# Two PSUM banks held as one tile, nine-row loads of q and k, and evictions with a stride, in an attention kernel followed by a hard-swish MLP

## The chip, the cores and the metric

One core of a Trainium2 chip. The metric is device time in microseconds (us). The kernel before took 399.7 us as the median of its first three runs.

## The reference, cut to what matters

```python
# q, k, v: (8, 8, 576, 64); s: (8, 8, 576); w_in: (512, 2048); w_out: (2048, 512)
cum    = np.cumsum(np.maximum(s, 0.0), axis=-1)
bias   = -(cum[:, :, :, None] - cum[:, :, None, :])
scores = np.where(causal, -1e9, q @ k.T / 8 + np.minimum(bias, 0.0))
attn   = softmax(scores)
x      = (attn @ v).transpose(0, 2, 1, 3).reshape(4608, 512)
h      = x @ w_in
out    = (h * np.clip(h + 3.0, 0.0, 6.0) / 6.0) @ w_out
```

64 heads are worked on as 32 pairs. For a pair, q and k are cast and transposed (qT, kT); scores gives exp(q k) in Pm; attend multiplies it by v into O, and VectorE divides by the row sums (r, then xs); x_transpose puts xs into xT, the x of the MLP. Four pairs give x for one batch of 576 tokens. The MLP runs in 9 blocks of 512 tokens; a block has 16 tasks `m1` (h, then in two steps, trl and gT, the hard-swish) and 16 tasks `m2` (a quarter of an output tile each).

Of the kernel before, what the change touches and what calls it, by code (L numbers as in the profile page):

```python
# [16 lines left out]
def kernel(  # L17
# [21 lines left out]
    NF = DFF // 128  # L39
    NBLK = NT // 512  # L40
    GRAN = 10
    VW = D + 2
    PW = 1664
    SLOTW = W2 + 64
# [2 lines left out]
    cpool = ctx.enter_context(tc.tile_pool(name="consts", bufs=1))  # L47
    work = ctx.enter_context(tc.tile_pool(name="work", bufs=2))
    psum = ctx.enter_context(tc.tile_pool(name="psum", bufs=1, space=bass.MemoryType.PSUM))

    ident_dram = nc.inline_tensor(np.eye(128, dtype=np.float16), name="ident_f16")

# [64 lines left out]
    qk_f = {}  # L117
    qk_h = {}

    def load_qk(p, eng):  # L120
        b, h0 = (2 * p) // H, (2 * p) % H
        t = work.tile([128, NTR, 2, D], F32, tag="qkf", bufs=3, name=f"qkf{p}")
        for i, src in enumerate((q, k)):
            eng.dma_start(
                out=t[:, :, i, :],
                in_=src[b, h0:h0 + 2].rearrange("h s d -> (h s) d").rearrange(
                    "(t p) d -> p t d", p=128
                ),
            )
        qk_f[p] = t  # L130

    def load_v(p, eng):
# [17 lines left out]

    def cast_qk(p):
        t = work.tile([128, NTR, 2, D], F16, tag="qkh", bufs=2)
        nc.gpsimd.tensor_copy(out=t, in_=qk_f.pop(p))  # L153
        qk_h[p] = t

    def cast_v(p):
        sl = p % NS
        eng = nc.vector if p in (1, 2, 3, 4) else nc.gpsimd
        eng.tensor_copy(out=v_h[:, sl, :, :, 0:D], in_=v_f[:, sl])  # L159

    def banks(early):

        return dict(tag="M", bufs=2) if early else dict(tag="S", bufs=3)

    def transpose_group(p, g):
        t0, t1 = ((0, 5), (5, 9))[g]
        n = (t1 - t0) * 128
        pT = psum.tile([128, 640], F16, **banks(p < 5))
        src = qk_h[p]
        for t in range(t0, t1):  # L170
            nc.tensor.matmul(  # L171
                out=pT[:, (t - t0) * 128:(t - t0 + 1) * 128],
                lhsT=src[:, t, :, :],
                rhs=ident,
                is_transpose=True,
                start=(t == t0),
                stop=(t == t1 - 1),
            )
        sl = p % NS
        c0 = t0 * 128  # L180
        nc.vector.tensor_copy(out=qT[0:64, sl, c0:c0 + n], in_=pT[0:64, 0:n])  # L181
        nc.vector.tensor_copy(out=kT[0:64, sl, c0:c0 + n], in_=pT[64:128, 0:n])  # L182
        if g == 1:
            qk_h.pop(p)



# [92 lines left out]
    def x_transpose(p):  # L280
        b, hp = p // (H // 2), p % (H // 2)
        xs = x_tiles.pop(p)
        pX = psum.tile([128, 640], F16, **banks(p < 3))
        for qt in range(5):
            nc.tensor.matmul(  # L285
                out=pX[:, qt * 128:(qt + 1) * 128],
                lhsT=xs[:, qt, :, :],
                rhs=ident,
                is_transpose=True,
                start=(qt == 0),  # L290
                stop=(qt == 4),
            )
        nc.vector.tensor_copy(out=xT[:, hp, b * SEQ:(b + 1) * SEQ], in_=pX[:, 0:SEQ])  # L293


    def load_w_in(c):
        nc.gpsimd.dma_start(
            out=w_in_sb[:, :, c * 512:(c + 1) * 512],
            in_=moe_w_in[:, c * 512:(c + 1) * 512].rearrange("(kc p) f -> p kc f", p=128),
        )  # L300

    def load_w_out(c):
        nc.gpsimd.dma_start(
            out=w_out_sb[:, c * 4:(c + 1) * 4, :],
            in_=moe_w_out[c * 512:(c + 1) * 512, :].rearrange("(ft p) j -> p ft j", p=128),
        )


    gT = {}
# [2 lines left out]
    def m1(n, f):  # L312
        if f == 0:
            gT[n] = work.tile([128, NF, 512], F16, tag="gT", bufs=2, name=f"gT{n}")
        ph = psum.tile([128, 512], F32, tag="M", bufs=2)
        for kc in range(KC):
            nc.tensor.matmul(  # L317
                out=ph,
                lhsT=w_in_sb[:, kc, f * 128:(f + 1) * 128],
                rhs=xT[:, kc, n * 512:(n + 1) * 512],  # L320
                start=(kc == 0),
                stop=(kc == KC - 1),
            )
# [5 lines left out]

    def m2(n, t4, part):  # L330
        if part == 0:
            pouts[n, t4] = psum.tile([128, 512], F32, tag="Y", bufs=1, name=f"po{n}_{t4}")
        po = pouts[n, t4]
        for f in range(4 * part, 4 * part + 4):
            nc.tensor.matmul(  # L335
# [13 lines left out]
    nc.vector.memset(bias3, 3.0)  # L349


    load_qk(0, nc.sync)
    load_v(0, nc.scalar)
    load_qk(1, nc.sync)
    load_v(1, nc.sync)
    load_qk(2, nc.sync)
    load_v(2, nc.sync)
    mask_rows(0, nc.scalar.copy)
    nc.scalar.activation(out=qaug, in_=c8, func=AF.Copy, scale=-1.0)
    mask_rows(1, nc.scalar.copy)  # L360
    nc.scalar.dma_start(
        out=kaug_dram.rearrange("r (h t) -> h r t", h=NH), in_=kaug
    )
    nc.scalar.dma_start(out=qaug_dram.rearrange("r (h t) -> h (r t)", h=NH), in_=qaug)
    load_aug(0, nc.scalar)
    load_aug(1, nc.scalar)


    def keep_warm(n):
        pw = psum.tile([128, 512], F32, tag="M", bufs=2, name="pw")  # L370
        for i in range(n):
            nc.tensor.matmul(
                out=pw, lhsT=warm[:, 0:128], rhs=warm, start=(i == 0), stop=(i == n - 1)
            )

    weights = {
        1: [(load_w_in, 0)],
        2: [(load_w_in, 1), (load_w_in, 2)],
        3: [(load_w_in, 3)],
        4: [(load_w_out, 0), (load_w_out, 1)],  # L380
        5: [(load_w_out, 2), (load_w_out, 3)],
    }

    def att_tasks(p):


        def loads():
            if p + 2 < NP:
                load_aug(p + 2, nc.sync)
            if p + 3 < NP:  # L390
                load_qk(p + 3, nc.sync)
                load_v(p + 3, nc.sync)
            for load, c in weights.get(p, []):
                load(c)

        more = p + 1 < NP
        tasks = [(loads, 0)]
        for bi in range(4):
            tasks.append((lambda bi=bi: scores_bank(2 * p, bi), 400))
        if p > 0:  # L400
            tasks.append((lambda: attend(2 * p - 1), 1200))
        if more:
            tasks.append((lambda: transpose_group(p + 1, 0), 640))
        for bi in range(4):
            tasks.append((lambda bi=bi: scores_bank(2 * p + 1, bi), 400))

        def casts():
            if more:
                cast_v(p + 1)
            if p + 2 < NP:  # L410
                cast_qk(p + 2)

        tasks.append((casts, 0))
        if p > 0:
            tasks.append((lambda: x_transpose(p - 1), 640))
        if more:
            tasks.append((lambda: transpose_group(p + 1, 1), 512))
        tasks.append((lambda: attend(2 * p), 1200))
        return tasks

    def weave(att, mlp):

        total = float(sum(c for _, c in att)) or 1.0
        done = 0.0
        for i, task in enumerate(mlp):
            while att and done / total < i / len(mlp):
                a, c = att.pop(0)
                a()
                done += c
            task()  # L430
        for a, c in att:
            a()

    def m1_tasks(n):
        return [lambda f=f: m1(n, f) for f in range(NF)]

    def m2_tasks(n):
        return [lambda t4=t4, part=part: m2(n, t4, part) for t4 in range(4) for part in range(4)]

    def merged(a, b):  # L440

        out_ = []
        for t in range(4):
            f, g = a[4 * t:4 * t + 4], b[4 * t:4 * t + 4]
            out_ += [g[0], g[1], f[0], g[2], f[1], g[3], f[2], f[3]]
        return out_

    keep_warm(22)
    cast_qk(0)
    transpose_group(0, 0)  # L450
    transpose_group(0, 1)
    mask_rows(2, nc.vector.tensor_copy)
    cast_v(0)
    cast_qk(1)
    keep_warm(10)
    att_all = []
    cut = []
    for b in range(B):
        for p in range(4 * b, 4 * b + 4):
            att_all += att_tasks(p)  # L460
            if p % 4 == 0:

                cut.append(len(att_all) - 2)
    att_all += [(lambda: attend(NH - 1), 1200), (lambda: x_transpose(NP - 1), 640)]
    cut.append(len(att_all))
    att_of = [att_all[cut[b]:cut[b + 1]] for b in range(B)]
    for task, _ in att_all[:cut[1]]:
        task()

    weave(att_of[1], m1_tasks(0))  # L470
    for n in range(NBLK - 1):
        att = att_of[n + 2] if n + 2 < B else []
        weave(att, merged(m1_tasks(n + 1), m2_tasks(n)))
    for task in m2_tasks(NBLK - 1):
        task()


# [28 lines left out]
```

## The kernel before: what the change and the argument touch

```python
def banks(early):
    return dict(tag="M", bufs=2) if early else dict(tag="S", bufs=3)

def load_qk(p, eng):                    # rows t*128 + partition: 256 bytes each
    t = work.tile([128, NTR, 2, D], F32, tag="qkf", bufs=3)
    for i, src in enumerate((q, k)):
        eng.dma_start(out=t[:, :, i, :], in_=src[...].rearrange("(t p) d -> p t d", p=128))

def transpose_group(p, g):              # five tiles of 128 rows, then four
    t0, t1 = ((0, 5), (5, 9))[g]
    n = (t1 - t0) * 128
    pT = psum.tile([128, 640], F16, **banks(p < 5))
    # ... one transpose for each t in t0..t1 ...
    nc.vector.tensor_copy(out=qT[0:64, sl, c0:c0 + n], in_=pT[0:64, 0:n])
    nc.vector.tensor_copy(out=kT[0:64, sl, c0:c0 + n], in_=pT[64:128, 0:n])

def m1(n, f):
    ph = psum.tile([128, 512], F32, tag="M", bufs=2)      # one bank, one tile
    for kc in range(KC):                                  # four matmuls
        nc.tensor.matmul(out=ph, lhsT=w_in_sb[:, kc, f * 128:(f + 1) * 128],
                         rhs=xT[:, kc, n * 512:(n + 1) * 512], ...)
    trl = work.tile([128, 512], F32, tag="trl", bufs=3)
    nc.scalar.activation(out=trl, in_=ph, func=AF.Relu, bias=bias3[:, 0:1], scale=1.0)
    nc.vector.scalar_tensor_tensor(out=gT[n][:, f, :], in0=trl, scalar=6.0, in1=ph,
                                   op0=ALU.min, op1=ALU.mult)

def m2(n, t4, part):
    if part == 0:
        pouts[n, t4] = psum.tile([128, 512], F32, tag="Y", bufs=1)
    # ... four matmuls; after the fourth part VectorE scales into osb, and osb goes out ...
```

Cut: scores, softmax, attend, the cumulative rows, and the order in which tasks are emitted.

The softmax here doesn't subtract the row's maximum and nothing guards it: scores larger than these inputs give would overflow.

## Time and profile before

| stretch of the kernel before | us | what sets its length |
|---|---|---|
| start to the first scores | 16.1 | the cumulative rows come back from DRAM |
| to the first m1 | 28.9 (until 45.0) | attention alone, GpSimd's casts, then a wait for q/k |
| to the second stage (first m2) | 37.5 (until 82.5) | m1 of block 0 woven with attention, one more wait for q/k |
| to the end | 314.8 (until 397.3) | TensorE, busy without a break |

The table cuts the span at four instructions: the first scores matmul, the first m1 matmul, the first m2 matmul of the second stage (after the change, the first beyond the eight m2 tasks that are moved forward), and the end. Two views that the prediction does not show are needed later. First, the groups of instructions of the kernel before, those of one m1 (columns: line, engine, operation, output and inputs, form, count; then busy time and the mean of one in ns; then the engine's idle time just ahead of the group and what ended most of it):

```profile
L317 PE MATMUL ph<-xT,w_in_sb 128*128 128x512 f16 x576 | 147.4, 381 | 0.0
L325 ACT ACTIVATE trl<-ph,bias 128x512 f32<-128x512 f32 x144 | 99.6, 692 | 82.8 <-PE ph L317 81.0 <-DVE kT L182 1.7
L326 DVE SCALAR_TENSOR_TENSOR gT<-trl,ph 128x512 f16<-128x512 f32 x144 | 98.8, 687 | 114.7 <-ACT trl L325 114.5
...
L317 PEld LDWEIGHTS <-w_in_sb 128*128 128x128 f16 x576 | 52.2, 98 | 44.5 <-issue 1.1
```

The last field of the first line is the one to watch: TensorE (PE) never waits for anything ahead of an m1, though each m1 is followed by 0.69 us on ScalarE (ACT) and 0.69 us on VectorE (DVE) that both read its bank.

### The profile page before, as it was taken

To read this page: it belongs to the slowest core of one execution; us is meant where nothing else is said; L and a number is where in the kernel's file an instruction comes from. 1 tells how busy PE (TensorE), PEld (TensorE's weight loads), DVE (VectorE), ACT (ScalarE), POOL (GpSimd) and SP (SyncE) were. 2 spreads that over 40 slices of the span, in tenths; PEclk is the share of its full clock that TensorE was granted. 3 is DMA by queue.
4 is the path that set the end of the run, shared out by engine and by line. 5 is a ranking of instruction groups with operands and counts; after the bars stand their busy time and mean duration, and the time that the engine had idled before them with its cause. 6 is when DMAs were issued, how large, how long until landed. Compare 5 with 4: busy or idle time off the path is not lost.

```text
span 397.3 us, 8194 instructions
## 1 busy us (share of the span) xinstructions
PE 366.4 (92%) x3040; PEld 209.7 (53%) x3040; DVE 227.2 (57%) x417; ACT 210.8 (53%) x406; POOL 140.3 (35%) x333
## 2 busy tenths in 40 slices
PE   7584776899999999999999999999999999999985
PEld 3363443555555555555555555555555544444432
DVE  4574372756666666666666666666665564454511
ACT  6364473755555566666666555555556633443400
POOL 3394825544444444444444444444443200000000
PEclk9999698999999999999999999999999999999999
DMA  9999999955555555554555455455100001010111
GB/s 176 201 213 205 185 208 178 194 108 118 116 118 118 119 117 118 119 117 117 118 118 118 108 126 114 109 126 116 38 28 27 28 26 54 26 53 28 49 58 54
DMA packets 123512, 43.40 MB, mean 109 GB/s; under 512 B 114192, under 2 KB 118672, under 8 KB 123472
## 3 DMA queue, kind: packets, MB, share of 16 engines
q1 hardware_dynamic: 117456, 37.89, 43.9%
q0 software_dynamic: 4224, 4.19, 6.4%
q10 hardware_dynamic: 1792, 0.79, 0.9%
q8 instruction: 24, 0.39, 0.4%
q14 instruction: 16, 0.13, 0.1%
HBM read 37.32 MB, written 9.73 MB: 118 GB/s over the span
## 4 chain that ended last, share of the span: by engine, by line
PE 80%; DMA 10%; POOL 4%; DVE 3%; ACT 2%; issue 1%; SPq 0%; POOLq 0%; ACTq 0%
PE po L335 31%; PE ph L317 29%; PE S L211 8%; DMA qkf<-in_k_dram 7%; PE O L260 6%; PE pT L171 3%; PE pX L285 2%; POOL Pm L224 2%; POOL t L153 1%; DMA kaug_scratch<-kaug 1%; DMA kT<-kaug_scratch 1%; ACT trl L325 1%; ACT Pm L219 1%; DMA s_sb<-in_s_dram 1%; DVE osb L344 1%; DVE gT L326 1%
## 5 line engine op out<-in xcount | busy, mean ns | idle before, releaser
L326 DVE SCALAR_TENSOR_TENSOR gT<-trl,ph 128x512 f16<-128x512 f32 x144 | 98.8, 687 | 114.7 <-ACT trl L325 114.5
L219 ACT ACTIVATE Pm<-S 128x384 f16<-128x384 f32 (+2 forms) x256 | 113.7, 506 | 80.3 <-PE S L211 72.5
L317 PE MATMUL ph<-xT,w_in_sb 128*128 128x512 f16 x576 | 147.4, 381 | 0.0
L335 PE MATMUL po<-w_out_sb,gT 128*128 128x512 f16 x576 | 144.4, 379 | 2.3 <-DVE osb L344 2.3
L325 ACT ACTIVATE trl<-ph,bias 128x512 f32<-128x512 f32 x144 | 99.6, 692 | 82.8 <-PE ph L317 81.0
L224 POOL TENSOR_SCALAR_AFFINE_SELECT Pm<-Pm 128x128 f16<-128x128 f16 (+2 forms) x256 | 78.8, 313 | 154.6 <-ACT Pm L219 144.8
L211 PE MATMUL S<-qT,kT 128*128 128x320 f16 (+4 forms) x448 | 71.4, 265 | 8.0 <-DMA kT<-kaug_scratch 3.0
L335 PEld LDWEIGHTS <-gT 128*128 128x128 f16 x576 | 51.2, 98 | 49.4 <-issue 3.2
L317 PEld LDWEIGHTS <-w_in_sb 128*128 128x128 f16 x576 | 52.2, 98 | 44.5 <-issue 1.1
L211 PEld LDWEIGHTS <-kT 128*128 128x128 f16 x448 | 42.1, 99 | 35.3 <-issue 4.9
L153 POOL CAST t<-qkf 128x1152 f16<-128x1152 f32 x32 | 36.7, 1147 | 21.4 <-DMA qkf<-in_k_dram 21.4
L260 PEld LDWEIGHTS <-Pm 128*128 128x128 f16 x960 | 37.4, 97 | 7.8 <-POOL Pm L224 1.6
L260 PE MATMUL O<-v_h,Pm 128*128 128x65 f16 x960 | 40.8, 193 | 0.5 <-POOL Pm L224 0.5
L171 PE MATMUL pT<-ident,t 128*128 128x128 f16 x288 | 26.8, 222 | 13.5 <-POOL t L153 12.9
L181 DVE COPY qT<-pT 64x640 f16<-64x640 f16 x64 | 28.3, 442 | 17.7 <-PE pT L171 17.6
L171 PEld LDWEIGHTS <-t 128*128 128x128 f16 x288 | 21.1, 99 | 28.1 <-POOL t L153 14.6
L344 DVE TENSOR_SCALAR osb<-po 128x512 f32<-128x512 f32 x36 | 24.8, 690 | 13.8 <-PE po L335 13.2
L182 DVE COPY kT<-pT 64x640 f16<-64x640 f16 x64 | 29.4, 459 | 0.9
L272 DVE TENSOR_TENSOR xs<-O,r 128x640 f16<-128x640 f32 x32 | 26.4, 824 | 1.1
L159 POOL CAST v_h<-v_f 128x640 f16<-128x640 f32 x28 | 20.1, 718 | 0.0
L285 PEld LDWEIGHTS <-xs 128*128 128x128 f16 x160 | 11.8, 99 | 10.9 <-issue 6.2
L293 DVE COPY xT<-pX 128x576 f16<-128x576 f16 x32 | 14.5, 453 | 1.7 <-PE pX L285 1.5
(29 smaller groups left out, 56.6 us busy)
## 6 DMA issues: line engine op xcount, KB each, us to landing
qkf<-in_q_dram SPq DMA_DIRECT2D x32, 288.0 KB
qkf<-in_k_dram SPq DMA_DIRECT2D x32, 288.0 KB
out_dram<-osb SPq DMA_DIRECT2D x36, 256.0 KB
v_f<-in_v_dram SPq DMA_DIRECT2D x62, 128.0 KB
w_in_sb<-in_moe_w_in_dram POOLq DMA_DIRECT2D x4, 512.0 KB, 8.1
w_out_sb<-in_moe_w_out_dram POOLq DMA_DIRECT2D x4, 512.0 KB, 10.1
v_f<-in_v_dram SPq DMA_DIRECT2D x31, 32.0 KB
kT<-kaug_scratch SPq DMA_DIRECT2D x30, 6.8 KB
```

Source lines behind the costliest of these rows:

```text
L153: nc.gpsimd.tensor_copy(out=t, in_=qk_f.pop(p))
L171: nc.tensor.matmul(out=pT[:, (t - t0) * 128:(t - t0 + 1) * 128], lhsT=src[:, t, :, :], rhs=ident, is_transpose=True, start=(t == t0), stop ...
L182: nc.vector.tensor_copy(out=kT[0:64, sl, c0:c0 + n], in_=pT[64:128, 0:n])
L211: nc.tensor.matmul(out=S[:, c:c + hi - lo], lhsT=kT[:, sl, off + 128 * kt:off + 128 * (kt + 1)], rhs=qT[:, sl, off + lo:off + hi], start=( ...
L219: nc.scalar.activation(out=P[:, p0:p0 + n], in_=S[:, 0:n], func=AF.Exp, scale=0.125, bias=0.0)
L224: nc.gpsimd.affine_select(out=view, in_=view, pattern=pattern, compare_op=ALU.is_ge, fill=0.0, base=0, channel_multiplier=-1,)
L260: nc.tensor.matmul(out=O[:, hh, qt * VW:qt * VW + D + 1], lhsT=P[:, c:c + 128], rhs=v_h[:, sl, hh, kt, 0:D + 1], start=(qt == 0), stop=(qt ...
L317: nc.tensor.matmul(out=ph, lhsT=w_in_sb[:, kc, f * 128:(f + 1) * 128], rhs=xT[:, kc, n * 512:(n + 1) * 512], start=(kc == 0), stop=(kc == ...
L325: nc.scalar.activation(out=trl, in_=ph, func=AF.Relu, bias=bias3[:, 0:1], scale=1.0)
L326: nc.vector.scalar_tensor_tensor(out=gT[n][:, f, :], in0=trl, scalar=6.0, in1=ph, op0=ALU.min, op1=ALU.mult)
L335: nc.tensor.matmul(out=po, lhsT=gT[n][:, f, t4 * 128:(t4 + 1) * 128], rhs=w_out_sb[:, f, :], start=(f == 0), stop=(f == NF - 1),)
L344: nc.vector.tensor_scalar_mul(out=osb, in0=po, scalar1=1.0 / 6.0)
```

## The change

Its intent: shorten the front, which waits for data. Five pairs of q and k are read with nine consecutive rows to a partition (2304 bytes in one piece instead of nine of 256). The transposes then give the tokens in another order, and the evictions put them right by reading PSUM with a step of 128 elements. For that, nine transposes (2304 bytes of 16-bit output a partition) need two adjacent banks, so the two M banks become one tile from which `bank()` hands out halves in turn. Besides, weights are loaded in larger rows (w_in's columns then come with a step of 8, by which m1 reads them), the first pair's cumulative rows go from SBUF to SBUF, loads are issued in another order, a pair's first transposes are emitted ahead of the attend of the finished pair (before: behind it), eight m2 tasks move into the first stage, and three output tiles use an M bank instead of Y.

```diff
+    Mt = psum.tile([128, 2, 512], F32, tag="M", bufs=1)
+    ring = [0]
+    def bank():
+        ring[0] ^= 1
+        return Mt[:, ring[0], :]
 def load_qk(p, eng):
+            if by_partition(p):                                  # p < PTN = 5
+                eng.dma_start(out=..., in_=rows.rearrange("(p t) d -> p t d", t=NTR))
+def transpose_pair(p):
+    pT = Mt.rearrange("p a b -> p (a b)").bitcast(F16)[:, 0:W2]
+    ...                                                          # nine transposes
+    for dst, r0 in ((qT, 0), (kT, 64)):
+        nc.vector.tensor_copy(
+            out=dst[0:64, sl, 0:W2].rearrange("d (p t) -> d p t", t=NTR),
+            in_=pT[r0:r0 + 64].rearrange("d (t p) -> d p t", p=128))
 def m1(n, f):
-        ph = psum.tile([128, 512], F32, tag="M", bufs=2)
+        ph = bank()
-                lhsT=w_in_sb[:, kc, f * 128:(f + 1) * 128],
+                lhsT=w_in_t[:, kc, f // 8, f % 8, :],            # columns 8 apart
 def m2(n, t4, part):
+            if (n, t4) in ((0, 1), (8, 1), (8, 3)):
+                pouts[n, t4] = bank()
     # cut: w_in in two loads of 4 KB rows, w_out in 8 KB rows, the order of loads,
     # pair 0's cumulative rows from SBUF to SBUF, eight m2 tasks in the first stage
```

## The prediction

> **What bounds the kernel now.** I read the page first: busy shares, then the forty slices.
>
> ```profile
> span 397.3 us, 8194 instructions
> PE 366.4 (92%) x3040; PEld 209.7 (53%) x3040; DVE 227.2 (57%) x417; ACT 210.8 (53%) x406; POOL 140.3 (35%) x333
> ...
> PE   7584776899999999999999999999999999999985
> ...
> PEclk9999698999999999999999999999999999999999
> DMA  9999999955555555554555455455100001010111
> ```
>
> TensorE (PE) is full from the ninth slice to the end. The first eight slices, 80 us, have holes in PE, and exactly there the DMA row is full. So two regimes: a front bound by data arriving, and a rear bound by PE, where only fewer PE cycles would help. Next the busy times by stretch, cut where the order of the work changes (columns: window, length, busy us and instructions of PE, PEld, DVE, ACT, POOL, then granted clock, DMA share, GB/s).
>
> ```profile
> 0.00:16.00 16.00, 9.62 (x41) 3.90 (x41) 7.65 (x13) 6.37 (x6) 4.64 (x12) 1.00 1.11 203
> 16.00:35.20 19.20, 15.90 (x234) 12.69 (x234) 13.08 (x29) 14.60 (x35) 16.24 (x39) 1.00 1.08 196
> 35.20:42.20 7.00, 0.15 (x5) 0.03 (x1) 1.23 (x3) 0.54 (x2) 1.14 (x2) 0.77 0.94 176
> 42.20:58.00 15.80, 14.51 (x144) 9.40 (x144) 9.95 (x20) 10.93 (x22) 9.97 (x23) 0.89 1.21 202
> 58.00:62.70 4.70, 0.09 (x1) 0.00 (x0) 1.04 (x2) 0.69 (x1) 1.16 (x2) 1.00 0.69 137
> 62.70:82.50 19.80, 17.77 (x170) 11.31 (x171) 13.07 (x25) 14.07 (x29) 10.21 (x26) 0.91 0.92 180
> 82.50:320.00 237.50, 237.50 (x2127) 140.53 (x2125) 149.29 (x281) 140.24 (x280) 96.89 (x232) 1.00 0.46 102
> ```
>
> The third and fifth rows are the holes: 7.0 and 4.7 us in which PE does nothing, and a lower clock in or after each. From 82.5 us PE is busy without a break. The waits say what ends the holes: the timeline of GpSimd (POOL) and PE, then the last m2 groups.
>
> ```profile
> 41.06 1.14 POOL L153 CAST t<-qkf 128x1152 f16<-128x1152 f32 x1 [7.27 <-DMA qkf<-in_k_dram]
> ...
> 42.26 0.71 PE L171 MATMUL pT<-ident,t 128*128 128x128 f16 x5 [6.91 <-POOL t L153]
> ...
> 61.54 1.15 POOL L153 CAST t<-qkf 128x1152 f16<-128x1152 f32 x1 [6.96 <-DMA qkf<-in_k_dram]
> ...
> 385.15 3.61 PE L335 MATMUL po<-w_out_sb,gT 128*128 128x512 f16 x16 [0.78 <-DVE osb L344]
> ```
>
> Twice a q/k pair comes late, its cast waits, PE waits for the cast. The last line is one of three equal 0.78 us waits at the very end, where the only Y bank must be evicted before the next output tile.
>
> **Unit costs from this trace.** Four 512-column matmuls start 0.86 us apart, so one m1 or m2 task is 0.86 us. A batch of the steady part (four head pairs, 16 m1, 16 m2) takes 237.5/6 = 39.6 us; its 32 tasks are 27.6, so attention is 12.0, or 3.0 us of PE a pair. In the window 82.5 to 320 PE hides everything else. DMA: in 340 to 360 us only output rows of 2 KB move, 40 GB/s at a share of 0.11, that is 364 GB/s at full share. In 120 to 280 us the share is 0.54 at 117 GB/s; a pair (9.9 us) moves 885 KB in 256-byte rows beside 262 KB of output, and 9.9 x 0.54 minus 0.72 for the output leaves 4.6 us: 192 GB/s. So 256-byte rows cost about twice as much per byte here.
>
> **What the Trainium skill says.** (1) "DMA: Bandwidth & Descriptors", Specifications: at least 512 B per transfer for line rate. The trace agrees (192 against 364 GB/s, just worked out). (2) "VectorE: DVE Perf Modes", What auto-detection actually checks: a 16-bit copy moves two per cycle only with step ±1 in every tensor. The contiguous evictions agree so far: the q copies of 640 and 512 elements take 476 and 408 ns, 128 elements per 68 ns, 1.9 per ns, and 136 ns fixed. The new ones read with a step of 128 elements, so I expect one per cycle of 0.96 GHz: 1152/0.96 + 136 = 1.34 us, an estimate; no run shows it yet. (3) "TensorE: Matmul & The Clock Gate", Weight-path perf modes: the fast weight load takes 32-column chunks packed or strided; so the new w_in weights with a step of 8 elements should load as before. (4) "SBUF — State Buffer", the note on cachelines: lines of 16 bytes, and a penalty where each access takes a new line; a step of 8 fp16 is just that. The two pull apart. The trace bounds the harm: these loads take 98 ns and matmuls start 216 ns apart, so even a doubled load hides.
>
> **The change part by part.**
>
> *Front, 0 to first scores (16.07 us before).* Pair 0's cumulative rows go from SBUF to SBUF instead of through DRAM (before: write 8.12 to 12.41, read back to 15.98 us). kaug is ready at 8.08; small copies land at about 10.5 to 11. But VectorE is busy with kaug until 8.1, and now has two 1.34 us evictions before anything reads kT: 10.8. The twelve warm-up matmuls then need a bank these evictions read, so they start at 10.8 and take 2.6: first scores at 13.4. Gain 2.6 us.
>
> *Attention alone, pairs 0 to 3 and both scores of pair 4 (19.1 us before).* GpSimd paced this before (the window 20 to 30 us has it busy 9.99 of 10). Its two larger w_in issues replace four, a little less work. VectorE gets more: per pair 2 x 1.34 = 2.7 us of eviction against 476+493+408+426 ns = 1.8, so 0.9 more, 4.5 us over five pairs. Worse is the order: a pair's nine transposes take both M banks, and x_transpose of the earlier pair needs one, so it cannot start until both evictions are done. Period of such a pair, from transposes done: 0.2 + 2.7 evictions, 0.4 x_transpose, 0.65 attend, 1.0 scores, 0.6 next transposes = 5.5 us. One pair at 4.7, three at 5.5, the half at 3.4: 24.6. Stage 1 starts at 38, 3 us later than before.
>
> *The loads.* Five pairs of q, k fall from 590 KB at 192 (3.1 us) to 590 KB at about 364 GB/s (1.6): 7.5 us less DMA. Weights now wait behind pair 3's and 4's casts, w_out behind the first m1. All work until pair 8 is loaded: q,k 5 x 1.6 + 4 x 3.1, v 9 x 1.5, weights about 25 (8.4 MB read at some 330 GB/s), other 3: 62 us. Pair 5 is issued near 29 and cast at 38, pair 6 issued near 34 and cast near 43. Neither should be late, so both holes, 11.7 us and the slow clock behind them, go.
>
> *Stage 1 (35.2 to 82.5, 47.3 us before).* Its PE work is 12.0 + 13.8 = 25.8. Now eight m2 tasks come in as well: 32.7. The first five m1 run with nothing between them on two banks: about 6 us instead of 4.3. Even without holes stage 1 had gaps (from 62.7 to 82.5 about a tenth), as four m1 a pair leave PE waiting for evictions. m2 tasks fill part of them. I take 36 us: stage 1 ends at 74.
>
> *Rear.* 397.3 - 82.5 = 314.8, less 6.9 for the m2 tasks already done, less 3 x 0.78 = 2.3 for the last tiles which now alternate between Y and M banks, plus 1.5 for a second stage thinner in tasks (24 for four pairs instead of 32): 307.1.
>
> Sum: 13.4 + 24.6 + 36 + 307.1 = 381 us of span. The measured time lies 1.7 to 2.4 us above the span (399.0 for the profiled run, median 399.7), so 383; as my estimates of the attention stage lean to the slow side, I take **382 us**, 4.4% less.
>
> **The rivals.** (a) *The strided evictions become the bound.* If a step of 256 bytes in PSUM costs more than one cycle an element, say 1.75, an eviction is 2.2 us, a pair 1.8 us more, and the first stage some 7 us longer: 389 to 391. For it: these evictions lie on the chain in the front, nothing hides them. Against: only five pairs. (b) *Same total, other hole.* The order of loads is one queue, and the cumulative rows of a later pair wait for PE; pairs 5 to 8 could be issued too late and the hole reappear under another name, or w_out arrive late at about 56 us. Then 388 to 395. For it: 62 us of DMA work must fit before about 62 us. Against: deadlines met with 5 us or more by my reckoning. (c) *Everything hides.* Attention alone keeps the old 4.4 us a pair and stage 1 runs at PE's pace: 13.4 + 20 + 34 + 306 = 373, so 375. (d) *Strided weights slow each m1*: 50 ns at each of 144 tasks is 7 us, in the rear, on the path. I think it unlikely.
>
> **Range and chances.** Low end near (c), high end at (a) or a mild (b): 374 to 391. Slower than 391.7 (2%) needs two of the rivals together: 9%. Slower by over 2% needs all, 1%.
>
> **What would show it.** Right: no wait of several us for q/k after 30 us; PE full from about 40 us on; strided evictions of 1.3 to 1.4 us; first scores near 13.4; stage 1 beginning near 38; clock 1.00 in the front; DMA share below 1 in places before 60 us; w_in weight loads still near 98 ns; no 0.78 us waits at the end. Wrong: evictions over 1.6 us, POOL casts waiting for q/k of pairs 5 to 8, or PE gaps after 75 us.

## More of the kernel before

Second, the chain that ended last, by engine, of the kernel before:

```profile
PE 80%; DMA 10%; POOL 4%; DVE 3%; ACT 2%; issue 1%; SPq 0%; POOLq 0%; ACTq 0%
```

## The result, and the profile after

The changed kernel took **475.2 us** (474.1 to 475.6, four runs), the kernel before 400.6 us in the same rounds. The ratio is 1.190, with a 95% interval of 1.181 to 1.199: 19% slower, where 4.4% less was predicted. Ratios here and below are the mean time of one kernel's fast runs over that of the other's in the same rounds, so they are not quite the ratios of the medians quoted.

The page of the changed kernel, as the prediction shows that of before:

```profile
span 472.3 us, 8189 instructions
## 1 busy us (share of the span) xinstructions
PE 380.5 (81%) x3038; PEld 237.6 (50%) x3038; DVE 234.2 (50%) x407; ACT 213.3 (45%) x406; POOL 137.8 (29%) x331
...
PE   5856666897878888888888888888888877677786
...
PEclk9889599999999999999999999999999999999999
DMA  4899963484444444444454454442000000100011
...
PE 58%; DVE 27%; ACT 11%; issue 3%; DMA 1%; ACTq 0%; DVEq 0%
```

TensorE has about the same work to do, but no slice after the ninth is full any more: 7 and 8 where there was 9, down to 6 and 7 at the far end, where nothing but the MLP runs. The clock is full there. DMA has gone from the chain (10% to 1%), as hoped; VectorE and ScalarE, 3% and 2% of the chain before, are now 27% and 11%. The groups of the changed kernel say which of their instructions:

```profile
L367 PE MATMUL Mt<-xT,w_in_sb 128*128 128x512 f16 x576 | 151.0, 385 | 71.4 <-DVE gT L376 69.8
...
L375 ACT ACTIVATE trl<-Mt,bias 128x512 f32<-128x512 f32 x144 | 99.0, 687 | 162.6 <-PE Mt L367 160.5
L376 DVE SCALAR_TENSOR_TENSOR gT<-trl,Mt 128x512 f16<-128x512 f32 x144 | 98.9, 687 | 199.3 <-ACT trl L375 199.3
L367 PEld LDWEIGHTS <-w_in_sb 128*128 128x128 f16 x576 | 80.5, 145 | 112.0 <-issue 84.4
...
L224 DVE COPY kT<-Mt 64x1152 f16<-64x1152 f16 x5 | 6.8, 1359 | 0.1
```

The three instructions of an m1 last as long as before, but TensorE is now idle for 71.4 us ahead of m1, 69.8 of them waiting for gT, the last reader of an M bank. That is most of the 75.0 us by which the span grew. The timeline of the changed kernel from 46 us, the lines of one m1 and the start of the next (start, length, engine, instruction, and in brackets the idle time before it and what ended it):

```profile
46.32 1.02 PE L367 MATMUL Mt<-xT,w_in_sb 128*128 128x512 f16 x4 [1.50 <-DVE gT L376]
...
47.38 0.69 ACT L375 ACTIVATE trl<-Mt,bias 128x512 f32<-128x512 f32 x1 [1.83 <-PE Mt L367]
...
48.10 0.69 DVE L376 SCALAR_TENSOR_TENSOR gT<-trl,Mt 128x512 f16<-128x512 f32 x1 [1.83 <-ACT trl L375]
...
48.84 1.69 PE L367 MATMUL Mt<-xT,w_in_sb 128*128 128x512 f16 x4 [1.50 <-DVE gT L376]
```

The three engines take turns. The matmuls, trl and gT follow one another, and only then does the next m1 begin: 48.84 - 46.32 = 2.52 us from one m1 to the next, though it writes the *other* bank. Before, an m1 had to wait only for the gT of two m1 earlier. A block of 16 m1 cannot then be shorter than 16 x 2.52 = 40.3 us. (In one stretch it was worse: from 47 to 59 us the granted clock was 0.59, and m1 tasks came 3.2 to 3.4 us apart.) In the last blocks, where no attention is left, one block took 40.6 us from its first m1 to the next block's, against 27.6 before. Where attention lies between the m1 tasks it fills part of the wait: a batch of four pairs takes 46.2 us, before 40.1. The same 40 us stretch in both, near the end (window, length, busy time and instructions of PE, PEld, DVE, ACT, POOL; clock; DMA share; GB/s), before and after:

```profile
320.00:360.00 40.00, 40.00 (x191) 18.30 (x190) 19.71 (x30) 15.84 (x23) 0.00 (x0) 1.00 0.11 40
```

```profile
320.00:360.00 40.00, 35.61 (x292) 22.50 (x290) 21.41 (x39) 20.82 (x40) 12.26 (x31) 1.00 0.07 23
```

The waits can be read in the built program too. Each engine has a semaphore that counts its finished instructions, and a matmul that has to wait names the count it waits for. With each count traced back to the instruction that brings it about:

```
                         first matmul of m1 that waits for gT     the gT is that of
before                   89 of 144                                 the m1 two before, in all 89
after                    141 of 144                                the m1 just before, in all 141
e1 (two tiles again)     80 of 144                                 the m1 two before, in all 80
e4 (before, one tile)    142 of 144                                the m1 just before, in all 142
```

(The others are covered by an earlier wait of the same engine.) So this was there to be read before any run. The prediction doesn't speak of these counts.

Where the time went, by the four cuts of the table above (us; the length of a stretch in brackets). The kernels from e1 on are those of the experiments:

| | first scores | first m1 | second stage | end |
|---|---|---|---|---|
| before | 16.1 | 45.0 (28.9) | 82.5 (37.5) | 397.3 (314.8) |
| predicted | 13.4 | 38 (24.6) | 74 (36) | 381 (307.1) |
| after | 15.7 | 43.7 (28.0) | 99.7 (56.0) | 472.3 (372.6) |
| e1, two tiles | 14.5 | 49.4 (35.0) | 88.7 (39.3) | 395.3 (306.6) |
| e13, two tiles, groups of 5 and 4 | 13.2 | 43.6 (30.4) | 84.4 (40.8) | 391.0 (306.6) |
| e7, as e13 with w_in and w_out as before | 14.6 | 45.4 (30.8) | 84.7 (39.3) | 389.8 (305.1) |
| e16, the best | 13.0 | 41.3 (28.3) | 80.5 (39.2) | 385.7 (305.2) |

Against before, the changed kernel lost 18.5 us in the first MLP stage and 57.8 in the rest, and gained 1.3 ahead of them. (Eight m2 tasks, 6.9 us, moved from the rest into that stage.) The rows come from different chips; e1 to e4, e6 to e9, e10 to e13, e14 to e16 ran side by side.

### The profile page after: what moved, and what is told of

The parts are those of the page before. It is cut to its first block, busy times and chain, and to the rows that moved or that the text cites. A ratio compares the mean times of both kernels' runs of the same rounds, so it can differ in the third digit from the quotient of the medians.

```text
span 472.3 us, 8189 instructions
## 1 busy us (share of the span) xinstructions
PE 380.5 (81%) x3038; PEld 237.6 (50%) x3038; DVE 234.2 (50%) x407; ACT 213.3 (45%) x406; POOL 137.8 (29%) x331
## 4 chain that ended last, share of the span: by engine, by line
PE 58%; DVE 27%; ACT 11%; issue 3%; DMA 1%; ACTq 0%; DVEq 0%
PE Mt L367 26%; PE po L389 17%; DVE gT L376 13%; ACT trl L375 10%; PE S L254 4%; DVE xs L315 4%; PE O L303 3%; DVE kT L210 2%; PE Mt L389 2%; DVE qT L210 2%; PE pT L328 2%; PE pT L195 2%; DVE kT L224 1%; DVE r L313 1%; PE Mt L409 1%
## 5 line engine op out<-in xcount | busy, mean ns | idle before, releaser
L367 PE MATMUL Mt<-xT,w_in_sb 128*128 128x512 f16 x576 | 151.0, 385 | 71.4 <-DVE gT L376 69.8
L376 DVE SCALAR_TENSOR_TENSOR gT<-trl,Mt 128x512 f16<-128x512 f32 x144 | 98.9, 687 | 199.3 <-ACT trl L375 199.3
L375 ACT ACTIVATE trl<-Mt,bias 128x512 f32<-128x512 f32 x144 | 99.0, 687 | 162.6 <-PE Mt L367 160.5
L367 PEld LDWEIGHTS <-w_in_sb 128*128 128x128 f16 x576 | 80.5, 145 | 112.0 <-issue 84.4
L389 PE MATMUL po<-w_out_sb,gT 128*128 128x512 f16 x528 | 133.2, 379 | 0.0
L254 PE MATMUL S<-qT,kT 128*128 128x320 f16 (+4 forms) x448 | 66.2, 263 | 3.9 <-ACT Pm L262 2.3
L254 PEld LDWEIGHTS <-kT 128*128 128x128 f16 x448 | 40.3, 98 | 25.9 <-DVE kT L224 1.4
L178 POOL CAST t<-qkf 128x1152 f16<-128x1152 f32 x27 | 31.0, 1148 | 0.0
L210 DVE COPY qT<-pT 64x640 f16<-64x640 f16 (+1 forms) x54 | 24.0, 445 | 4.8 <-PE pT L195 4.2
L210 DVE COPY kT<-pT 64x640 f16<-64x640 f16 (+1 forms) x54 | 24.8, 460 | 0.7
L409 PE MATMUL Mt<-warm 128*128 128x512 f16 x30 | 10.1, 511 | 4.4 <-DVE kT L224 3.1
```

The costliest lines, as they stand in the source:

```text
L178: nc.gpsimd.tensor_copy(out=t, in_=f.rearrange("p (t i d) -> p t i d", i=2, d=D))
L210: nc.vector.tensor_copy(out=dst[0:64, sl, c0:c0 + n], in_=pT[r0:r0 + 64, 0:n])
L254: nc.tensor.matmul(out=S[:, c:c + hi - lo], lhsT=kT[:, sl, off + 128 * kt:off + 128 * (kt + 1)], rhs=qT[:, sl, off + lo:off + hi], start=( ...
L367: nc.tensor.matmul(out=ph, lhsT=w_in_t[:, kc, f // 8, f % 8, :], rhs=xT[:, kc, n * 512:(n + 1) * 512], start=(kc == 0), stop=(kc == KC - 1),)
L389: nc.tensor.matmul(out=po, lhsT=gT[n][:, f, t4 * 128:(t4 + 1) * 128], rhs=w_out_sb[:, f, :], start=(f == 0), stop=(f == NF - 1),)
```

## The experiments

**The theory**: the single tile makes two banks act as one, which costs about 75 us, and what remains is a small gain. **The rivals**: the strided weight loads slow m1 (they rose from 98 to 145 ns), or the new order of loads and the strided evictions did it. Fifteen kernels were run (there is no e5); all gave correct results.

| kernel | us, median | before, same rounds | ratio (95%) |
|---|---|---|---|
| e1 | 398.2 | 399.6 | 0.996 (0.992 to 1.001) |
| e2 | 474.4 | 399.6 | 1.189 (1.182 to 1.195) |
| e3 | 396.6 | 399.6 | 0.993 (0.989 to 0.998) |
| e4 | 470.0 | 399.6 | 1.176 (1.170 to 1.182) |
| e6 | 393.7 | 399.2 | 0.987 (0.983 to 0.990) |
| e7 | 389.9 | 399.2 | 0.977 (0.973 to 0.981) |
| e8 | 394.7 | 399.2 | 0.990 (0.986 to 0.994) |
| e9 | 393.9 | 399.2 | 0.987 (0.983 to 0.991) |
| e10 | 397.2 | 400.7 | 0.993 (0.988 to 0.998) |
| e11 | 401.0 | 400.7 | 1.003 (0.995 to 1.011) |
| e12 | 407.0 | 400.7 | 1.017 (1.011 to 1.023) |
| e13 | 392.2 | 400.7 | 0.979 (0.973 to 0.985) |
| e14 | 391.1 | 397.6 | 0.987 (0.980 to 0.995) |
| e15 | 396.3 | 397.6 | 0.998 (0.989 to 1.007) |
| e16 | 386.7 | 397.6 | 0.975 (0.968 to 0.982) |

In the call of e14 to e16, two runs of the kernel before fell in the slow state; they are not in the ratios, but in the median of 397.6.

### e1, e2, e3, e4: the tile against the weights

e1 is the changed kernel with two tiles of one bank, in turn:

```diff
-    Mt = psum.tile([128, 2, 512], F32, tag="M", bufs=1)
     def bank():
-        ring[0] ^= 1
-        return Mt[:, ring[0], :]
+        return psum.tile([128, 512], F32, tag="M", bufs=2, name="Mb")
     # transpose_pair: eight transposes in one tile, the ninth in the next; four evictions
```

> The changed kernel with the two M banks given out as two separate tiles again (each transposed pair takes both, its evictions are split 8+1). In the built program an m1 then waits for the eviction of the m1 two before it, not of the one just before. Theory A (one two-bank tile makes every m1 wait for the last one's eviction): 378 to 392 us, the 69 waits of m1 on the gT eviction gone. Theory B (the w_in weights with a step of 8 elements slow m1): stays above 440 us. Theory C (strided evictions and the longer front are the loss): above 450 us, as nothing of them is changed.

e2 keeps the tile and takes back the weights:

```diff
-                lhsT=w_in_t[:, kc, f // 8, f % 8, :],
+                lhsT=w_in_sb[:, kc, f * 128:(f + 1) * 128],
     # and w_out in rows of 2 KB, as before
```

> The changed kernel with w_in read in 128 adjacent columns again (and w_out loaded to match); the one two-bank tile stays. Theory A: within 10 us of the changed kernel, 465 to 476 us; the w_in weight loads fall from 145 to 98 ns but the waits on gT stay. Theory B: below 410 us.

e3 is both edits.

> Two separate M tiles and w_in in adjacent columns together. Theory A: within 4 us of the kernel with two tiles alone if strided weight loads hide behind the 216 ns matmuls; if each m1 pays about 50 ns for the stride on the path, 5 to 9 us less than it. Theory B alone: same as dense weights alone.

e4 goes the other way: the kernel *before*, with nothing but the tile changed (the m1, warm-up and early transpose buffers of before become halves of one tile):

```diff
-        ph = psum.tile([128, 512], F32, tag="M", bufs=2)
+        ph = bank()            # half of the one [128, 2, 512] tile, in turn
```

> The kernel before with one thing changed: its two M banks become one two-bank tile with alternating halves. Theory A: slower by a good part of 75 us, 440 to 480 us, with m1 waiting on gT every time. Theories B and C: no change, 397 to 402 us.

Measured: undoing the tile takes 77 us away (e1 against the changed kernel) and undoing the weights alone takes nothing (e2, 474.4). The tile alone makes the kernel before 70 us slower (e4). The waits of TensorE for gT, first in e1, then in e4 (engine, line, releaser; us in total, times, longest):

```profile
PE Mb L368 <- DVE gT L377: 2.1, 3, 0.8
```

```profile
PE Mt L325 <- DVE gT L334: 59.7, 80, 2.0
```

The stretch near the end, for e4:

```profile
320.00:360.00 40.00, 34.85 (x297) 19.81 (x295) 19.59 (x37) 19.65 (x38) 10.17 (x28) 1.00 0.06 21
```

Where TensorE was busy for all 40 us before, it now loses 5, as in the changed kernel, and attention is still running at 320 us (GpSimd, POOL, has work). The cause of the slowdown is shown from both sides. But with it undone, e1 and e3 gain only 0.4% (not clear of zero) and 0.7%, not 4.4%, so something else in the prediction failed as well. The further runs look for that.

### e6, e7, e9: is the nine-row form worth it?

All three have two tiles and the weights as before. e6 also loads all pairs in rows of 256 bytes, as before the change, with the evictions that go with that:

```diff
-    PTN = 5
+    PTN = 0
```

> Two M tiles and dense weights as in the kernel with both, and all pairs read row by row with plain evictions in two halves (no nine-row pairs). Theory D (the strided evictions, which stand in front of the xs product in VectorE's order, are what lengthens the attention-alone stage from 19 to over 30 us): that stage falls back to about 20 us, total 381 to 386. Theory E (nine-row loads are needed so that the data arrives): holes with casts waiting for q/k come back and the total stays at 392 to 400.

e7 keeps the nine-row loads but transposes in groups of five and four, with one tile each, so that no eviction of a ninth transpose is left over:

```diff
+        for t0, t1 in ((0, 5), (5, 9)):
+            pT = bank().bitcast(F16)
+            ...                                            # transposes t0..t1
+            for dst, r0 in ((qT, 0), (kT, 64)):
+                o = dst[0:64, sl, 0:W2].rearrange("d (p t) -> d p t", t=NTR)
+                nc.vector.tensor_copy(out=o[:, :, t0:t1],
+                    in_=pT[r0:r0 + 64, 0:n].rearrange("d (t p) -> d p t", p=128))
```

> As the kernel with both, but each nine-row pair is transposed in groups of 5 and 4 on one bank each with a strided eviction each (about 0.80 and 0.67 us), in place of 8 and 1 (1.22 and 0.70). Theory D: 0.9 us less VectorE a pair and an earlier start of the first eviction, so 4 to 6 us less, 390 to 393. Theory E: no change, 396.

e9 is e6 without the twelve warm-up matmuls ahead of the first scores:

```diff
-    keep_warm(12)
```

> The row-by-row version without the twelve warm-up matmuls before the first scores. They took 4.4 us on the path at a lowered clock and waited for the first evictions. If they are pure cost: 3 to 4 us less than the version with them. If they keep the clock up for what follows: no gain or a loss, with a granted clock under 0.8 from 12 to 30 us.

e7 is 2.3% faster than before, e6 1.3%, e9 no different from e6. The loads in rows of 256 bytes bring a wait back under another name. The timeline of e6, TensorE, from 34 us:

```profile
41.17 1.19 PE L255 MATMUL S<-qT,kT 128*128 128x256 f16 x5 [6.18 <-DMA kT<-kaug_scratch]
```

Now the cumulative rows of a later pair come late, issued behind q and k on the same queue: the prediction's rival (b). With nine-row loads this wait is gone (e7), so that part of the change does what it was meant for. e7's attention stage is still 30.8 us where 24.6 was predicted. Its timeline from 28 us shows why (VectorE's order, and what TensorE waits for):

```profile
28.80 0.82 DVE L222 COPY qT<-Mb 64x640 f16<-64x640 f16 x1 [2.28 <-PE Mb L191]
...
31.19 0.72 DVE L222 COPY kT<-Mb 64x512 f16<-64x512 f16 x1
...
31.94 0.22 DVE L309 RECIPROCAL r<-O 128x10 f32<-128x10 f32 x1
32.19 0.82 DVE L311 TENSOR_TENSOR xs<-O,r 128x640 f16<-128x640 f32 x1
...
33.08 0.45 PE L324 MATMUL Mb<-ident,xs 128*128 128x128 f16 x5 [2.53 <-DVE xs L311]
```

Four evictions take VectorE from 28.80 to 31.91. The r and xs of the finished pair stand behind them in VectorE's program and end at 33.01; then x_transpose can start, and TensorE has waited 2.53 us. This happens at each of three pairs. The prediction's period counted the evictions and what follows on TensorE, but not r and xs, 1.04 us, which sit on the same chain.

### e8: the moved tasks alone

e8 is the kernel before with the eight m2 tasks moved forward and three output tiles on M banks (as separate tiles):

```diff
-    weave(att_of[1], m1_tasks(0))
+    weave(att_of[1], m1_tasks(0) + m2_0[:8])
+    weave(att_of[2], merged(m1_tasks(1), m2_0[8:], 2))
     # and po of (0, 1), (8, 1), (8, 3) from tag "M", bufs=2
```

> The kernel before with two parts alone: eight of the first m2 tasks moved into the first MLP stage, and three output tiles on M banks. If the moved tasks fill gaps that are not waits for data, up to 6.9 us, and the three 0.78 us waits go, 2.3 us: 389 to 395. If the first stage is bound by the two holes only, the tail alone: 396 to 398.

1.0% faster: this harmless part of the change brings nearly half of what e7 gains.

### e10, e11, e12: taking r and xs out from behind the evictions

e10 is e7 with the evictions of k on ScalarE; e11 is e7 with attend (and so r and xs) emitted ahead of the first transposes of the next pair, as in the kernel before, for all pairs; e12 has both.

```diff
-                nc.vector.tensor_copy(out=o[:, :, t0:t1], ...)
+                copy = nc.scalar.copy if r0 else nc.vector.tensor_copy      # e10, e12
+                copy(out=o[:, :, t0:t1], ...)
-        a += here[0] if here else []
         a += [(lambda: attend(2 * p - 1), 1200)] if p > 0 else []
+        a += here[0] if here else []                                        # e11, e12
```

> As the 5 and 4 split, with the strided evictions of k given to ScalarE and those of q left on VectorE. Theory D (xs waits behind 2.9 us of strided evictions in VectorE's order, a pair takes 7 us in the attention-alone stage): VectorE has 1.5 us less before xs and a pair falls to about 5.5 us, so 5 to 7 us less, 383 to 385. Rival E2 (the data is then late, as with rows by tile): no more than 2 us less, with waits for cumulative rows or q/k over 3 us.

> As the 5 and 4 split, with the attend of the earlier head issued ahead of the next pair's transposes, as the kernel before has it; so xs comes ahead of the strided evictions in VectorE's order. Theory D: the 2.5 us waits of x_transpose for xs go; part of them comes back as scores waiting for kT; 2 to 5 us less, 385 to 388. Rival: no change, 390, if the evictions themselves and not their place set the pace.

> Both: k evictions on ScalarE and attend first. Theory D: a pair near 4.6 us in the attention-alone stage, 380 to 384. Rival E2: 386 to 390 with a new wait for data between 30 and 60 us.

None is faster than e7. e11's attention stage is shorter, 27.2 us against 30.8, so the reading of the order is right. But in the steady part, where TensorE had hardly waited, scores now wait: 16 times for the exponent (Pm) on ScalarE, 6.7 us in all, and 4 times for kT, 2.9 us. A batch of four pairs takes 42.25 us instead of 39.92: the rear grows by 11.6 us. In e10 the first scores come later (17.3 us), then q and k of a later pair come 5.4 us late, and the second stage begins at 89.4 us instead of e7's 84.7. Both orders together are the slowest.

### e13: the weights once more, without the uneven evictions

e13 is e7 with the strided w_in and the 8 KB w_out of the change: its only differences to the changed kernel are the two tiles and the groups of five and four.

```diff
     # e7, and again:
+                lhsT=w_in_t[:, kc, f // 8, f % 8, :],
```

> The 5 and 4 split with the changed kernel's own weight layout (w_in read with a step of 8 elements, w_out in 8 KB runs). If strided weight loads hide: within 2 us of the dense version (389.9). If each m1 pays for the stride, up to 7 us more.

The weight loads of m1, first in e13, then in e7:

```profile
L363 PEld LDWEIGHTS <-w_in_sb 128*128 128x128 f16 x576 | 76.7, 146 | 33.5 <-issue 3.9 <-DMA w_in_sb<-in_moe_w_in_dram 1.7
```

```profile
L361 PEld LDWEIGHTS <-w_in_sb 128*128 128x128 f16 x576 | 52.2, 98 | 49.0 <-issue 4.4
```

146 ns against 98, yet a batch takes 40.22 us against 39.92: 0.30 us over 16 m1, 19 ns of each. Over the whole rear it is 1.5 us (306.6 against 305.1). e7 and e13 ran on different chips; e1 and e3, which differ by the same edit and ran side by side, give 306.6 against 305.2. So the rival (d) exists at a fifth of its size.

### e14, e15, e16: the order for the early pairs only, and what comes late then

e14 is e7 with attend first for the first four pairs only. e15 is e14 with nine-row loads for nine pairs (the transposes of the added four go into S banks). e16 is e14 with the four w_out loads issued behind later m1 tasks.

```diff
-        a += here[0] if here else []
-        a += [(lambda: attend(2 * p - 1), 1200)] if p > 0 else []
+        at = [(lambda: attend(2 * p - 1), 1200)] if p > 0 else []
+        t0 = here[0] if here else []
+        a += at + t0 if p < 4 else t0 + at                  # e14, e15, e16
-    PTN = 5
+    PTN = 9                                                 # e15
-    for c, f in enumerate((0, 2, 5, 8)):
+    for c, f in enumerate((4, 7, 10, 13)):                  # e16
```

> The 5 and 4 split with attend first for pairs 0 to 3 only. The first m1 should start at 40 us, as with attend first everywhere (45.4 without), and a batch in the steady part take 40.0 us again. Theory D alone: the 5 us stay, 385. Theory E2 as well: a cast waits about 5 us for q/k near 60 us, block 1 starts only some 3 us earlier, 387.

> The same with nine-row loads and strided evictions for nine pairs instead of five. Theory E2: four pairs' q and k cost half the DMA time, 6 us less, so the wait near 60 us goes and block 1 starts at 80 to 81: 383 to 385. Against: 0.9 us more VectorE for each of these pairs beside m1's evictions: no gain over five pairs.

> Attend first early, five pairs, and the four w_out loads issued behind m1 tasks 4, 7, 10, 13 in place of 0, 2, 5, 8. Theory E2 (w_out competes with q/k of pair 7): the wait near 60 us goes, block 1 at 80 to 81, 383 to 385. If w_out is then itself late: m2 waits for it near 70 us, no gain.

In e14 the attention stage shrinks to 27.8 us, and the first MLP stage grows to 43.1: what was won is waited for again. Its timeline from 56 us, GpSimd and TensorE:

```profile
61.89 1.15 POOL L174 CAST t<-qkf 128x1152 f16<-128x1152 f32 x1 [4.25 <-DMA qkf<-in_k_dram]
...
63.10 0.45 PE L191 MATMUL pT<-ident,t 128*128 128x128 f16 x5 [2.34 <-POOL t L174]
```

q and k of a pair compete with the w_out loads and come late. e16 issues w_out later and this wait is gone: the stage takes 39.2 us again, the start is kept, and the kernel takes 386.7 us, 2.5% less than before. This is the shortest time found, and it beats both kernels; its ratio alone does not tell it apart from e7's, but beside e14, in the same rounds, it is 4.4 us faster. More nine-row pairs (e15) don't help in another way: scores wait up to 2.7 us for a strided kT eviction and m1 up to 1.8 us for gT; the first MLP stage takes 48.5 us. Nearly all the waits of TensorE there name VectorE or ScalarE, not the loads.

## Why the prediction was wrong

**The step that failed** is in "The change part by part". *Stage 1* takes it that m1 runs "on two banks", and *Rear* gives the M banks no cost at all. In the changed kernel two banks remain, but one tile holds them, and the waits are kept by tile. The runs showed at least 2.52 us from one m1 to the next instead of the 0.86 us that TensorE needs, 40.6 us for one of the last blocks instead of 27.6, and 46.2 us for a batch with attention instead of the predicted 39.6. The first five m1, which *Stage 1* allowed about 6 us, took 13.5 us in the changed kernel (43.73 to 57.26) and 6.1 in e16, with two tiles. The rear came to 372.6 us instead of 307.1, stage 1 to 56.0 instead of 36: 85.5 of the 91.3 us by which the predicted span was wrong (4.8 of them, in stage 1, stay with two tiles, as e13 shows below). None of the rivals (a) to (d) was this one; all of them lay in the front or in the weights, and the chance of "slower" followed from them. The Trainium skill, "PSUM — Partial Sum Buffer", section "PSUM bank collisions raise a hardware error", advises to guard PSUM by bank and quadrant, "by bank is the simple version". The trace agrees that a bank is enough: with a guard by bank (e1, e13) the results were correct and the waits short. Here the guard spanned two.

The rest can be judged on e13, which differs from the changed kernel only by two tiles and groups of five and four. It takes 392.2 us; its stages add up to a span 10.0 us over the predicted one:

- **Front, 13.4 us predicted, 13.2 in e13, 15.7 in the changed kernel.** The strided evictions were right: 1.36 us, predicted 1.34. So what the Trainium skill, "VectorE: DVE Perf Modes", section "What auto-detection actually checks", says of the step held: reading PSUM with a step of 256 bytes lost the two-per-cycle rate and little more. The warm-up was not right: in the changed kernel, twelve matmuls took 4.44 us instead of 2.6. The timeline, TensorE, at 11 us, and the stretch around it (clock after the five busy times):

```profile
11.46 4.44 PE L409 MATMUL Mt<-warm 128*128 128x512 f16 x12 [3.06 <-DVE kT L224]
```

```profile
11.46:15.70 4.24, 4.24 (x12) 1.60 (x12) 0.80 (x2) 0.81 (x1) 1.81 (x2) 0.60 0.77 168
```

  TensorE had stood idle for 3.06 us and was granted 0.60 of its clock. The Trainium skill, "TensorE: Matmul & The Clock Gate", section "What's actually happening", gives idle windows of about 3.4 us as the cause of half the clock; the trace agrees in kind, 370 ns a matmul here against 233 in the same place before (2.33 us for ten), after an idle time of 0.86 us. But the length of this wait alone doesn't decide it: e7 and e13 have the same front and both idle 2.00 us there, and the twelve matmuls took 4.31 us in e7 (first scores at 14.6) and 2.76 in e13. That e13 comes so near to 13.4 is thus partly luck. Without these matmuls nothing is gained, though (e9, on the row-by-row form).

- **Attention alone, 24.6 us predicted, 30.4 in e13, 28.0 in the changed kernel.** This is the larger of the two terms that were mis-sized, by 5.8 us. A pair took 7.8 and 6.6 us in e7 (from one x_transpose to the next), not 5.5. Left out were r and xs, 1.04 us, behind the evictions on VectorE; and in groups of five and four the evictions take 3.1 us instead of 2.7. That makes 6.9. The changed kernel itself shows the missing term best: its evictions take the 2.7 us reckoned, and the pair from 33.19 to 39.65 us, at a granted clock of 1.00, took 6.46 us, where 5.5 + 1.04 is 6.54. The granted clock, 0.78 in this stage of e13, is likely to hold part of what is left, but no run tells that apart. e14 shortened this stage by 3.0 us by moving r and xs ahead.

- **Stage 1, 36 us predicted, 40.8 in e13, 39.2 in e16.** The idle time was about right: in e16 TensorE waits 3.8 us there, and 36 - 32.7 = 3.3 was allowed. The work was not: TensorE was busy 35.3 us, not 32.7. The stage holds the transposes of five pairs and not of four, but these nine are worth only some 0.8 us (in the trace of before, from 82.5 to 320 us, 202 of them keep TensorE busy for 18.6 us); the rest stays open.

- **The loads.** Right that nine-row loads are needed and that the two holes for q and k go (e6 against e7). Half right that nothing else would be late: as soon as the front gets faster, q and k are late again (e14), the mild form of rival (b). Issuing w_out later removes that wait (e16), so it was w_out that stood in the way.

- **Rear, 307.1 us predicted.** 305.1 in e7, 306.6 in e13 and e1. The moved tasks and the alternating last tiles worked about as reckoned; e8, which has them alone, has a rear of 308.0 us and is 1.0% faster as a whole.

- **Strided weights.** Predicted near 98 ns, measured 146. Right was the bound drawn from the trace: a load that stays well under the 216 ns between matmuls hides nearly all of it.

With the failed step taken out, the nearest kernels measured are e13, 392.2 us (2.1% less than before), and e1, whose evictions are cut into eight and one, 398.2 us: at most half of the gain of 4.4%, in the direction predicted. With the failed step in, no part of the sum could save the answer.

## What to carry to other kernels

Count tiles, not banks: in this program buffers rotate and free one another by tile (e1, e4), so when a change merges two buffers into one object to get a contiguous view, every user of that object loses its double buffering. That is worth checking wherever a chain of engines, here 2.52 us of matmul, trl and gT, is hidden only by the second buffer; look for the *count* that a wait names, not only for the engine. And in a front that several engines and loads share, a gain of a few microseconds in one place can turn into a wait for the next late load (e6, e10, e14), so measure the parts one by one and move the load that gets in the way.

## What the Trainium skill lacked or had wrong

- "PSUM — Partial Sum Buffer", section "PSUM bank collisions raise a hardware error", says by what to guard PSUM but not what a coarser guard costs. Here a guard over two banks instead of one took an m1 from 0.86 to 2.52 us, and the kernel from 399.6 to 470.0 us (e4).
- "TensorE: Matmul & The Clock Gate", section "Weight-path perf modes", names packed and strided chunks side by side with no cost for columns a step apart. With a step of 8 16-bit elements a load took 146 ns instead of 98, of which 19 ns an m1 of four loads reached the time.
- "SBUF — State Buffer", the note on cachelines, warns of a penalty for each access to a new line without a size. The runs show two costs of steps of 16 bytes or more, though not that the lines cause them: 146 against 98 ns for these weight loads, and evictions that write single elements 18 bytes apart (64x128 in 0.70 to 0.72 us in e1), while evictions in runs of five to nine elements cost about 1.05 ns an element over a fixed 0.14 us (64x640 in 0.82 us, 64x1152 in 1.35).
